# Contiguous stationary operands for the row maxima, and the row of maxima sent in four transfers

## The chip, the cores and the metric

The kernel runs on one core of a Trainium2 chip. The metric is the device time of one execution in microseconds (us). Before the change the median of three runs is 927.35 us (926.88 to 927.9).

## What is computed

An attention with queries pooled in pairs, followed by a two-layer block with a squared ReLU. Cut to what matters:

```
q, k, v: (4, 8, 1152, 64)
q_pool = q.reshape(B, H, S // 2, 2, D).mean(axis=3)
scores = scale * q_pool @ k^T
scores = scores - max(scores, axis=-1)
attn = exp(scores); attn = attn / (attn.sum(-1) + 1e-9)
x = (attn @ v), heads side by side: (2304, 512)
h = x @ w_in; r = maximum(h, 0); g = s * r * r + b
out = g @ w_out: (2304, 512)
```

There are 32 heads (4 batches of 8). The change touches only the maxima that are subtracted from the scores: one number for each of the 576 pooled queries of each head.

## The kernel before, in words

The work has two stages. The attention goes over 16 pairs of heads and takes somewhat more than the first half of the span; the two-layer block follows. The order of the work is written out by hand: a loop over 288 steps (32 heads of 9 blocks of 128 keys), in which strings of letters say in which order a step's score products, value products and maximum products are issued.

In a step, `score_step` (line 740) makes the scores of 128 keys against the 576 queries of a head: four matmuls on TensorE (PE), two for each half of the queries. In the first of the two the high parts are multiplied, and the second adds the low parts and, through one row of `qq` that meets a row of -1 in `kk`, subtracts the maxima. ScalarE (ACT) takes the exponentials (L749, L752), VectorE (DVE) or GpSimd (POOL) makes their low parts (L755), and `value_step` (L772 to L782) multiplies them with the values three steps later.

The maxima of a pair of heads are made while the pair before is worked on, by `max_unit`: 27 products for a pair, each of 128 queries against 384 keys, one PE matmul (L685) and one DVE reduction (L686). The stationary operand (the weights of the matmul) is a block of queries. In three of the 27 products it is `qm`, the last 64 queries of both heads; in the other 24 it is a quarter of `qz`, which holds the first 512 queries of one head with zeros beside them. For the first two pairs `qz` is written in an order in which a quarter is 128 neighbouring columns. From the third pair on a transfer copies `qh` into `qz` as it is (L591), and a quarter is read with a step of four columns of four bytes: quarter t holds the queries t, t + 4, t + 8 and so on. So the maxima of partition m lie beside one another in `pm` in the order of the queries.

When a head's maxima are complete, `shift` reduces them to `c` (L720 on DVE), and one tick later two transfers carry `c` into the row of `qq` that the second score matmul reads: the first 512 (L725, 128 partitions of four elements) and the last 64 (L726). Both are issued from the queue of SyncE (SP), which issues its transfers in the order of the program: a transfer that has to wait for its data holds up all that stand behind it. In the same queue stand the loads of raw keys and queries of the pair three further on (L546, L554), the copies of `kh`, `kT`, `qh` and `qT` into `kk` and `qq` (L609 to L630), the loads of the values (L559), the queries for the maxima (L591), the weights of the second stage (L202) and the results (L821). Twice in a pair the queue comes to a row of maxima.

Below, "the row" of a head is this row of maxima, and heads are counted from 0: head 4 is the first of the third pair.

Of the kernel before, what the change touches and what calls it, by code (L numbers as in the profile page):

```python
# [56 lines left out]
def f32(ap):  # L57
    return ap.bitcast(F32)
# [3 lines left out]
def attention_moe_kernel(ctx: ExitStack, tc: tile.TileContext, q, k, v, w_in, w_out, s_in, b_in, out):  # L62
    nc = tc.nc
    B, H, S, D = q.shape
# [4 lines left out]
    P = 128  # L69
# [3 lines left out]
    NT4 = SQ // P  # L73
# [228 lines left out]
    def later(k, fn):  # L302
        step[1] += 1
        queue.append((step[0] + k, step[1], fn))
# [215 lines left out]
    qzs = [ap.tile([P, 2, NT4 * P], F32R, name=f"qz{i}") for i in range(2)]  # L520
# [148 lines left out]
    def max_unit(u, pool, tag):  # L669

        p, w = divmod(u, NU)
        t, e = divmod(w, NE) if u >= (NT4 + 1) * NE else divmod(w, NT4 + 1)[::-1]
        if w == 0:
            pms[p] = ap.tile([P, NJ, NE], F32, tag="pm", bufs=2, name=f"pm{p}")
        h = 0 if t <= NT4 else 1
        ps = pool.tile([P, 512], F32, tag=tag, name=f"m{p}_{w}") if tag == "m" else pool.tile([P, 2, 512], F32, tag=tag, name=f"m{p}_{w}")[:, 0]
        if t == 0:
            assert holds["qm"] == p  # L680
            st, col = qm, NT4
        else:
            st = qzs[p % 2][:, h].rearrange(*(("p (m t) -> p t m",) if p > 1 else ("p (t m) -> p t m",)), t=NT4)[:, (t - 1) % NT4]
            col = (t - 1) % NT4 + h * (NT4 + 1)
        nc.tensor.matmul(ps[:, :KB], st, khs[p][:, e * KB:(e + 1) * KB], start=True, stop=True)  # L685
        nc.vector.tensor_reduce(out=pms[p][:, col, e:e + 1], in_=ps[:, :KB], axis=AX.X, op=ALU.max)  # L686
        if e == NE - 1 and t and t % NT4 == 0:
            pm = pms[p] if h == 0 else pms.pop(p)
            shift(2 * p + h, pm[:, h * NT4:(h + 1) * NT4 + 1], slice(0, NT4) if h == 0 else slice(1, NT4 + 1), NT4 if h == 0 else 0)
# [10 lines left out]
    def shift(hd, pm, full, rest):  # L700


        if hd == 0:
            turned = ap.tile([P, (NT4 + 1) * 32], F32, name="turned")
            nc.vector.tensor_reduce(out=first.rearrange("p (t i) -> p t i", i=32)[:, :, 0], in_=pm, axis=AX.X, op=ALU.max)
            nc.vector.transpose(out=turned, in_=first)
            flat = qqs[0].rearrange("p i a n -> p (i a n)")[D:D + 1, NT4 * P:].rearrange("p (t q i) -> p t q i", q=4, i=32)
            for g in range(4):
                at = flat[:, 0:NT4 + 1, g + 2] if g < 2 else flat[:, 1:NT4 + 1, g - 2]
                src = turned[32 * g:32 * g + 1].rearrange("p (t i) -> p t i", i=32)[:, :NT4 + 1 if g < 2 else NT4]  # L710
                if g % 2:
                    nc.scalar.activation(at, src, AF.Copy)
                else:
                    nc.vector.scalar_tensor_tensor(out=at, in0=src, scalar=1.0, in1=src, op0=ALU.mult, op1=ALU.max)
            holds["c", 0] = 0
            return
        c = ap.tile([P, 32], F32R, tag="c", bufs=2, name=f"c{hd}")[:, :NT4 + 1]
        row = qqs[hd % 3][:, 1].rearrange("p a n -> p (a n)")
        h = hd % 2
        nc.vector.tensor_reduce(out=c, in_=pm, axis=AX.X, op=ALU.max)  # L720

        eng = nc.sync

        def send():
            eng.dma_start(f32(row[D:D + 1, :NT4 * P]), f32(c[:, full]))  # L725
            eng.dma_start(f32(row[D:D + 1, NT4 * P:]), f32(c[h * D:(h + 1) * D, rest:rest + 1]))  # L726
            holds["c", hd % 3] = hd

        later(1, send)
# [136 lines left out]
    for n in range(AHEAD):  # L866
        for u in range(begun(n - AHEAD), begun(n - AHEAD + 1)):
            max_unit(u, *((ps_m, "m") if u % 2 == 0 else (ps_s, "s")))
            if u == 1:
                prep["qz1"]()  # L870
                load_q(1, (1,))
                load_k(1)
                load_q(1, (0,))
                prep["l1"]()
                zeros(1)
                constants(1)
                prep_v(0)
                ones(1)
                constants(2)
        tick()  # L880
        if n == 11:
            prep = prep_pair(1)
# [6 lines left out]
    for n in range(NS + LAG):  # L889
        hd, j = divmod(n, NJ)  # L890
# [4 lines left out]
        for part in ORDS.get(n % 18, ORD[at]) if at is not None else "sff":  # L895
            if part == "s" and n < NS:
                score_step(hd, j, KIND[n % 18])
            elif part == "f":
                for u in units:
                    max_unit(u, ps_m, "m")  # L900
                    break
            elif part == "v":
                if products is None:
                    products = value_step(*divmod(n - LAG, NJ))
                next(products)
# [3 lines left out]
        if n < NS:  # L909
            p, h = divmod(hd, 2)  # L910
# [150 lines left out]
```

## Time and profile before

| | |
|---|---|
| median of the runs | 927.35 us (926.88 to 927.9) |
| the profiled execution's own time | 927.01 us |
| its span, first to last instruction | 925.0 us |
| mean granted TensorE clock | 0.999 |
| PE matmul busy | 901.7 us (97%) |
| DVE, ACT, POOL busy | 692.1, 649.3, 631.0 us |
| matmuls of the maxima, L685 | 432 |
| transfers of rows of maxima, L725 and L726 | 31 and 31 |

Busy time of PE is modelled from the ends of its matmuls, which overlap, so 97% says that PE seldom stood without a matmul, not that it ran at its best. What one matmul costs is better read from the start of the one behind it. The weight loads are listed apart, as PEld; they lie beside the matmuls before them. "SPq" rows are transfers being issued: their length is the time in which SP was busy with the issue, and the landing comes later.

### The profile page before, as it was taken

The numbers are of one execution on the slowest core, as the hardware profiler recorded it, in microseconds if no ns is written. First come the engines' busy times: TensorE is split into PE (matmuls) and PEld (weight loads), VectorE is DVE, ScalarE is ACT, GpSimd is POOL, SyncE is SP. The second block draws the span as 40 slices with busy tenths as digits, with TensorE's granted clock in tenths as the row PEclk, the third lists the DMA queues.
The fourth block names the chain that finished last, engine by engine and source line by source line (L and its number), as shares of the span: only waits on it lengthen the run. The fifth ranks groups of instructions, "written<-read, shape, count | busy, mean of one in ns | idle before, by whom it ended". The sixth has DMA issues, their size and how long they took to land.

```text
span 925.0 us, 17875 instructions
## 1 busy us (share of the span) xinstructions
PE 901.7 (97%) x6164; PEld 864.3 (93%) x6164; DVE 692.1 (75%) x1272; ACT 649.3 (70%) x1209; POOL 631.0 (68%) x503
## 2 busy tenths in 40 slices
PE   5999999999999999999999999999999999999997
PEld 3898999999999999999998899989999999999997
DVE  6877878888888888888876587788884556666656
ACT  4878788888888888888888776756664444454443
POOL 7966866777777777777757566659997345555543
PEclk9999999999999999999999999999999999999999
DMA  9799887887788778777671367656653322222111
GB/s 162 152 183 194 181 185 147 174 182 175 152 176 181 172 149 186 174 172 150 140 177 50 124 186 227 216 158 219 205 167 109 114 69 69 69 70 69 47 47 46
DMA packets 257977, 134.65 MB, mean 146 GB/s; under 512 B 204192, under 2 KB 227872, under 8 KB 257888
## 3 DMA queue, kind: packets, MB, share of 16 engines
q1 hardware_dynamic: 250784, 132.63, 59.5%
q10 hardware_dynamic: 7104, 0.89, 0.6%
q8 instruction: 50, 0.82, 0.4%
q14 instruction: 39, 0.32, 0.1%
HBM read 68.68 MB, written 18.87 MB: 95 GB/s over the span
## 4 chain that ended last, share of the span: by engine, by line
PE 89%; POOL 3%; DMA 2%; DVE 2%; ACT 2%; issue 1%; SPq 0%; ACTq 0%; POOLq 0%; DVEq 0%
PE s L740 15%; PE h L412 11%; PE y L387 11%; PE h L360 10%; PE m L685 10%; PE seven L456 10%; PE o L778 7%; PE o L782 7%; PE o L780 6%; PE o L772 3%; POOL pl L755 1%; DMA kraw<-in_k_dram 1%; DMA kk<-kh 1%; ACT ph L749 0%; DMA qraw<-in_q_dram 0%
## 5 line engine op out<-in xcount | busy, mean ns | idle before, releaser
L686 DVE TENSOR_REDUCE pm<-m 128x1 f32<-128x384 f32 x432 | 230.8, 548 | 65.4 <-PE m L685 53.7
L755 POOL TENSOR_TENSOR pl<-pe,ph 128x576 fp32r<-128x576 f32 x128 | 182.0, 1432 | 103.2 <-ACT pe L752 77.1
L749 ACT ACTIVATE ph<-s 128x576 fp32r<-128x576 f32 x256 | 166.3, 650 | 73.3 <-PE s L740 67.7
L740 PE MATMUL s<-qq,kk 128*128 128x288 f32 x1152 | 202.4, 297 | 4.7 <-DVE pl L755 2.4
L740 PEld LDWEIGHTS s<-qq,kk 128*128 128x128 f32 x1152 | 174.4, 190 | 8.4 <-issue 1.9
L685 PE MATMUL m<-kh,qz 128*128 128x384 f32 x384 | 171.4, 454 | 0.3 <-DVE pm L686 0.3
L782 PE MATMUL o<-pl,vv 128*128 128x288 f32 x512 | 151.2, 295 | 1.2 <-POOL pl L755 1.2
L780 PE MATMUL o<-ph,vl 128*128 128x288 f32 (+1 forms) x512 | 150.9, 295 | 0.3 <-POOL vl L660 0.3
L778 PE MATMUL o<-ph,vv 128*128 128x288 f32 x512 | 150.8, 295 | 0.0
L685 PEld LDWEIGHTS m<-kh,qz 128*128 128x128 f32 x384 | 115.1, 300 | 5.4 <-DVE pm L686 2.3
L755 DVE TENSOR_TENSOR pl<-s,ph 128x576 fp32r<-128x576 f32 x128 | 96.4, 753 | 29.0 <-ACT s L752 22.1
L360 PE MATMUL h<-x,wih 128*128 128x256 f32 x576 | 106.8, 283 | 1.1 <-DVE gl L374 1.0
L412 PE MATMUL h<-x,wih 128*128 128x256 f32 x576 | 104.2, 281 | 0.0
L782 PEld LDWEIGHTS o<-pl,vv 128*128 128x128 f32 x512 | 96.7, 189 | 6.8 <-POOL pl L755 1.5
L360 PEld LDWEIGHTS h<-x,wih 128*128 128x128 f32 x576 | 93.7, 190 | 8.0 <-DVE gl L374 2.2
L778 PEld LDWEIGHTS o<-ph,vv 128*128 128x128 f32 x512 | 97.0, 190 | 0.0
L440 POOL TENSOR_TENSOR cl<-c,ch 128x640 fp32r<-128x640 f32 x35 | 55.0, 1571 | 56.3 <-ACT ch L436 56.3
L412 PEld LDWEIGHTS h<-x,wih 128*128 128x128 f32 x576 | 88.7, 188 | 0.2
L780 PEld LDWEIGHTS o<-ph,vl 128*128 128x128 f32 (+1 forms) x512 | 86.3, 169 | 0.6 <-POOL vl L660 0.6
L752 ACT ACTIVATE s<-s 128x576 f32<-128x576 f32 x128 | 83.1, 649 | 0.0
L752 ACT ACTIVATE pe<-s 128x576 f32<-128x576 f32 x128 | 82.9, 648 | 0.0
L360 PE MATMUL h<-x,wil 128*128 128x256 f32 x288 | 81.6, 283 | 0.0
(294 smaller groups left out, 2058.4 us busy)
## 6 DMA issues: line engine op xcount, KB each, us to landing
kk<-kh SPq DMA_DIRECT2D x31, 576.0 KB, 6.5
vf<-in_v_dram SPq DMA_DIRECT2D x32, 288.0 KB, 3.9
qq<-qh SPq DMA_DIRECT2D x64, 144.0 KB, 6.1
xr<-xd SPq DMA_DIRECT2D x18, 512.0 KB, 3.8
kk<-kT SPq DMA_DIRECT2D x31, 288.0 KB, 4.4
qraw<-in_q_dram SPq DMA_DIRECT2D x120, 72.0 KB, 2.5
kraw<-in_k_dram SPq DMA_DIRECT2D x60, 144.0 KB, 3.1
wsti<-in_moe_w_in_dram SPq DMA_DIRECT2D x13, 512.0 KB, 4.0
```

Of the source, the lines that this page charges most:

```text
L360: nc.tensor.matmul(h[:, :TB], st[:, c, :], mv[:, c, :], start=(n == 0), stop=(n == 3 * NC - 1))
L387: nc.tensor.matmul(y[:, :DM], st[:, ts_], mv, start=(first and n == 0), stop=(last and n == 2))
L412: nc.tensor.matmul(h[:, e * TB:(e + 1) * TB], st[:, c, :], mv[:, c, :], start=(k == 0), stop=(k == 3 * NC - 1))
L685: nc.tensor.matmul(ps[:, :KB], st, khs[p][:, e * KB:(e + 1) * KB], start=True, stop=True)
L686: nc.vector.tensor_reduce(out=pms[p][:, col, e:e + 1], in_=ps[:, :KB], axis=AX.X, op=ALU.max)
L740: nc.tensor.matmul(ps[:, a, :HALF], kk[:, i, j * P:(j + 1) * P], qq[:, i, a], start=(i == 0), stop=(i == 1))
L749: nc.scalar.activation(ph, ps[:, :, :HALF], AF.Exp, scale=SCALE)
L752: nc.scalar.activation(full, ps[:, :, :HALF], AF.Exp, scale=SCALE)
L755: fresh.append(lambda: eng.tensor_tensor(out=pl, in0=full, in1=f32(ph), op=ALU.subtract))
L778: nc.tensor.matmul(o[:, :HALF], vv[:, j], ph[:, a], start=first, stop=False)
L780: nc.tensor.matmul(o[0:vl.shape[2], :HALF], vl[:, j], ph[:, a], start=False, stop=False)
L782: nc.tensor.matmul(o[:, :HALF], vv[:, j], pl[:, a], start=False, stop=last)
```

## The change

The quarter of `qz` is now 128 neighbouring columns, so quarter t holds the queries 128 t to 128 t + 127. Nothing is changed in what fills `qz`: the first two pairs keep their reordered copy, the others get the queries in their natural order. In `c`, column t then holds the maxima of 128 neighbouring queries, one in each partition. From head 4 on the row is therefore sent in four transfers of 128 elements of four bytes, one for each column; the transfer of the last 64 stays as it was. Heads 1 to 3 keep their one transfer (head 0 has another way).

```diff
@@ max_unit
-            st = qzs[p % 2][:, h].rearrange(*(("p (m t) -> p t m",) if p > 1 else ("p (t m) -> p t m",)), t=NT4)[:, (t - 1) % NT4]
+            st = qzs[p % 2][:, h, (t - 1) % NT4 * P:((t - 1) % NT4 + 1) * P]
@@ shift, send
-            eng.dma_start(f32(row[D:D + 1, :NT4 * P]), f32(c[:, full]))
+            if hd < 4:
+                eng.dma_start(f32(row[D:D + 1, :NT4 * P]), f32(c[:, full]))
+            else:
+                for t in range(NT4):
+                    eng.dma_start(f32(row[D:D + 1, t * P:(t + 1) * P]), f32(c[:, full.start + t:full.start + t + 1]))
             eng.dma_start(f32(row[D:D + 1, NT4 * P:]), f32(c[h * D:(h + 1) * D, rest:rest + 1]))
```

On PE, DVE, ACT and POOL the instructions stand in the order in which they stood. The SP queue gets three more transfers for each of 28 heads, 84 in all. This is the queue at heads 4 and 5, where it changes first; `kraw` and `qraw` are raw keys and queries, `qz` the queries for the maxima (the numbers behind names are the program's own and shift by themselves):

```order
-L725 DMA qq_98<-c_1036 1x128x4
-L726 DMA qq_98<-c_1036 1x64x1
-L546 DMA kraw_1088<-in_k_dram 32x36x32 x4
-L554 DMA qraw_1093<-in_q_dram 32x18x32 x8
+L729 DMA qq_98<-c_1036 1x128x1 x4
+L730 DMA qq_98<-c_1036 1x64x1
+L546 DMA kraw_1091<-in_k_dram 32x36x32 x4
+L554 DMA qraw_1096<-in_q_dram 32x18x32 x8
 L591 DMA qz_102<-qh_961 64x512 x2
-L725 DMA qq_99<-c_1235 1x128x4
-L726 DMA qq_99<-c_1235 1x64x1
```

Everything behind a row, here the raw loads and `qz`, now stands behind three more transfers. The second place is one pair in the queue of the changed kernel, from the row of an even head (8) over the one of the odd head (9) to the load of values behind it (`wsti` is a weight of the second stage, `vf` the values):

```order
L729 DMA qq_99<-c_1934 1x128x1 x4
L730 DMA qq_99<-c_1934 1x64x1
L546 DMA kraw_1989<-in_k_dram 32x36x32 x4
L554 DMA qraw_1994<-in_q_dram 32x18x32 x8
L591 DMA qz_102<-qh_1859 64x512 x2
L202 DMA wsti0b<-in_moe_w_in_dram 128x2x256
L729 DMA qq_97<-c_2144 1x128x1 x4
L730 DMA qq_97<-c_2144 1x64x1
L559 DMA vf_104<-in_v_dram 128x9x64
```

The values of an odd head stand directly behind that head's row, and behind them (not shown) the copies into `kk` and `qq` for the next pair; these too are three transfers later.

## Rows read from the trace of the kernel before

**Rows 1.** Windows: length, busy PE, PEld, DVE, ACT, POOL, clock, DMA share, GB/s

```profile
50.76:85.05 34.29, 31.69 (x206) 30.32 (x205) 25.64 (x47) 25.37 (x47) 22.60 (x16) 1.00 0.93 193
...
333.75:364.83 31.08, 31.08 (x205) 30.46 (x204) 25.88 (x49) 26.32 (x50) 23.63 (x19) 1.00 0.81 169
```

**Rows 2.** Line 685, 62 to 494.5 us: count, duration min/median/max in ns

```profile
L685 PEld LDWEIGHTS m<-kh,qz x335: 308/309/314, 62.6 to 494.1; 128*128 128x128 f32 x168
...
L685 PEld LDWEIGHTS m<-kh,qm x39: 187/188/188, 91.0 to 466.0; 128*128 128x128 f32 x39
```

**Rows 3.** Timeline of PE (start, length in us): second pair's quarter, then a later one

```profile
43.26 0.33 PE L685 MATMUL m<-kh,qz 128*128 128x384 f32 x1
43.43 0.29 PE L778 MATMUL o<-ph,vv 128*128 128x288 f32 x1
...
253.09 0.43 PE L685 MATMUL m<-kh,qz 128*128 128x384 f32 x1
253.36 0.30 PE L782 MATMUL o<-pl,vv 128*128 128x288 f32 x1
```

**Rows 4.** Timeline of PE: the same behind an L772 matmul, second pair, then a later one

```profile
44.28 0.55 PE L685 MATMUL m<-kh,qz 128*128 128x384 f32 x1
44.67 0.69 PE L740 MATMUL s<-qq,kk 128*128 128x288 f32 x4
...
358.18 0.55 PE L685 MATMUL m<-kh,qz 128*128 128x384 f32 x1
358.57 0.69 PE L740 MATMUL s<-qq,kk 128*128 128x288 f32 x4
```

**Rows 5.** Timeline of the SP queue: start, length of the issue

```profile
336.74 0.54 SPq L202 DMA_DIRECT2D wsto1b<-in_moe_w_out_dram  x1
340.10 0.51 SPq L725 DMA_DIRECT2D qq<-c  x1
340.65 0.59 SPq L726 DMA_DIRECT2D qq<-c  x1
341.34 0.54 SPq L559 DMA_DIRECT2D vf<-in_v_dram  x1
...
357.03 0.51 SPq L725 DMA_DIRECT2D qq<-c  x1
```

**Rows 6.** Waits of the SP queue, 81 to 450.3 us: total, times, longest

```profile
SPq L725 <- DVE c L720: 44.8, 24, 3.5
SPq L612 <- PE m L685: 5.6, 15, 0.8
```

**Rows 7.** Lines 725 and 726, whole span: issue in ns min/median/max; landing of L726

```profile
L725 SPq DMA_DIRECT2D qq<-c x31: 482/510/1344, 29.6 to 495.5; - x31
...
L726 SPq DMA_DIRECT2D qq<-c x31: 588/594/1397, 30.2 to 496.1; - x31
...
DMA to landing us min/median/max: 1.8/1.8/3.1
```

**Rows 8.** Timeline of PE: the first score matmuls of heads 4 and 22

```profile
85.05 0.69 PE L740 MATMUL s<-qq,kk 128*128 128x288 f32 x4
...
364.83 0.69 PE L740 MATMUL s<-qq,kk 128*128 128x288 f32 x4
```

**Rows 9.** Waits of PE, 50.76 to 92 us

```profile
PE s L740 <- DMA qq<-c: 0.7, 1, 0.7
```

**Rows 10.** Timeline of SP: the last transfer of the row of head 4

```profile
81.79 0.59 SPq L726 DMA_DIRECT2D qq<-c  x1
```

**Rows 11.** Timeline of ACT: values of heads 3 and 21 rounded, idle time before in brackets

```profile
70.45 0.69 ACT L293 ACTIVATE vv<-vf 128x576 fp32r<-128x576 f32 x1 [3.24 <-DMA vf<-in_v_dram]
...
349.32 0.69 ACT L293 ACTIVATE vv<-vf 128x576 fp32r<-128x576 f32 x1
```

**Rows 12.** DMA issues of the page: size, median us to landing

```profile
vf<-in_v_dram SPq DMA_DIRECT2D x32, 288.0 KB, 3.9
```

**Rows 13.** DMA queue of the page: packets, MB, share of 16 engines' span

```profile
q1 hardware_dynamic: 250784, 132.63, 59.5%
```

## The prediction, made before the changed kernel was run

> **What bounds the kernel now.** I read the windows first, because shares of the whole span mix two stages and the change lies in the attention alone. In a pair from the middle, PE is busy for all of 31.08 us [rows 1]; ACT has 26.32, DVE 25.88, POOL 23.63, and the transfers take 0.81 of the 16 DMA engines. So PE sets the pace of a pair, with some 5 us to spare on the others. In the second pair PE stands idle for 2.6 of 34.29 us, 0.7 of it for a row of maxima [rows 1, 9].
>
> Then I looked at line 685 by stationary operand. A load of `qm`, which is contiguous, takes 188 ns; one of a strided quarter of `qz` takes 309 [rows 2]. Loads lie beside matmuls, so their length alone says little. The timeline gives the price: from a strided product to the next matmul PE takes 0.27 us; from the same product in the second pair, where the quarter is contiguous, 0.17 [rows 3].
>
> Last I read the SP queue, the only one that the change lengthens. It is nearly as full as PE. From one row to the next, 340.10 to 357.03, it issues without a long pause; ahead of the row at 340.10 it stands from 337.28 on, for its data [rows 5]. From head 4 to head 28 it waits 44.8 us in 24 waits for `c` [rows 6], 1.9 us for a head, and this is nearly all the room that it has.
>
> **What the change takes away.** 14 pairs have 24 strided products each, 336. Not all of them gain. Three in a pair stand between an L772 matmul and a score matmul, and there the step is 0.39 us with the contiguous quarter too (44.28 to 44.67) as with the strided one (358.18 to 358.57) [rows 4]: the load is not what is waited for. I cost these 42 at nothing. The other 21 in a pair gain 0.27 - 0.17 = 0.10 us: 2.1 us for a pair, which would then take 29.0. ACT would be busy for 26.3 of these, DVE for 25.9: tight, but not the bound. If only PE mattered, the pairs behind head 4 would give 13 x 2.1 = 27 us.
>
> The row shows the strided load 121 ns dearer than the contiguous one. The Trainium skill, page "SBUF — State Buffer", section "Door 1: The DMA port swizzle", gives 4 fp32 as the step that is still free, which is this step; by that sentence the change would take nothing away. The trace does not agree: 309 against 188 ns.
>
> **What it adds.** Three transfers for each of 28 heads, all on SP. The trace of before has none of 128 elements of four bytes. Its neighbours are L725 (128 partitions, 0.51 us to issue) and L726 (four-byte elements, 0.59 us) [rows 7]; from one start to the next it is 0.55 and, by the two transfers behind 340.65, at most 0.69 [rows 5]. I take 0.60, the new one being like the one in its partitions and like the other in its elements: a = 1.8 us for a head, 3.6 for a pair. The ends are 0.55 (a = 1.65) and 0.69 (a = 2.07). Nothing covers this but the waits of SP itself.
>
> On the DMA engines a row becomes 512 packets instead of 128: 768 more in a pair. At the mean of the queue, 0.595 x 925 x 16 / 250784 = 35 ns a packet [rows 13], these are 1.7 us of the 16 engines in a pair, an upper bound since the mean holds packets of kilobytes. With 0.81 x 31.08 = 25.2 us that makes 26.9 of 29.0. I cost it at nothing; PE and SP cover it.
>
> **The sum.** In a pair SP had 3.7 us of waits for `c` and gets 3.6 us of issues, while PE wants to be 2.1 us faster. Both can't be had: SP becomes the bound, and the rows arrive late, where now they arrive early. Head 22 shows how early: its last transfer leaves at 357.59 (0.56 behind L725), lands 1.8 us later at 359.4, and the head begins at 364.83 [rows 5, 7, 8]: 5.4 us of slack. Once this is used up, PE waits at the even heads until the row has landed.
>
> So I follow SP. Up to the row of head 4 I take it as full, since PE was short of a row there already [rows 9], and nothing moves. From there to head 28 it loses its waits and gains the issues: 44.8 + 2 - 24 x 1.8 = 3.6 us earlier. The 2 are my estimate for the waits on buffers that PE frees, of which L612 alone has 5.6 [rows 6]; an SP that is late meets fewer of them. The row of head 28 lands 3.6 - 1.8 earlier, and PE, with no slack left, starts the head 5.4 + 1.8 = 7.2 us earlier than now. Behind that SP has no raw loads any more, and PE gains the 2.1 us of the last pair's products. Together 9.3 us; the second stage just starts so much sooner. At head 4 itself PE loses: the last transfer left at 81.79 [rows 10], leaves 1.8 us later and lands at 85.4 to 86.7 by the ends of its landing time [rows 7], where the head began at 85.05 [rows 8]. That loss is inside the count, since SP is what is followed.
>
> Against the profiled execution, 927.0 us, this gives 917.7; I say **918**. The median of the runs is 0.3 above that execution, well inside the range. In short the gain is 54.3 - 25 a: 13 us at a = 1.65, 2.5 at 2.07, and 2 less where the other waits do not shrink. The forecast's own range is 908 to 926.
>
> What is late next: the values of an odd head stand behind its row. At head 21 they leave at 341.34, land 3.9 us later at 345.2 and are rounded by ACT at 349.32 [rows 5, 11, 12]: 4.1 us of slack, which loses 1.8 and then what SP is late. How it looks when it is gone stands at 70.45, where ACT idles 3.24 us for it [rows 11]. I expect a microsecond there at odd heads, paid out of the wait that PE would have at the next even head.
>
> **The rivals.**
> *PE stays the bound.* If SP's smaller waits, on buffers that PE frees, vanish as well, or the added issues come at the cheap end, SP keeps up. For it: L612 is only one of several lines that wait so. Against it: by the formula a would have to be 1.1, or 0.37 a transfer, unless some 18 us of such waits go. Then the full 27 us come, less 1 at head 4: about 901.
>
> *The added issues cost more than the two neighbours.* It turns at 54.3 = 25 a, that is a = 2.17, 0.72 us for an added transfer. For it: both lines have issues of 1.3 and 1.4 us [rows 7], when the queue ahead of them is full, and an SP that never pauses will find it full more often; in the second pair, with a DMA share of 0.93, PE was already short of a row [rows 1, 9]. Against it: the medians lie close to the minima. With 0.9 us a transfer, between 0.6 and 1.2, a is 2.7 and the kernel is 13 us slower, 940.
>
> *The loads don't get faster*, because the step is not what makes them slow. For it: the strided loads also follow transfers into `qz`, those of the first two pairs do not. Against it: the same line, shape and engine, with 188 ns in the second pair's step of 0.17. Then PE keeps 31.08 a pair, SP fits under it with 3.6 for 3.7 us, and the wait at head 4 remains: 928. The sentence on the step in the Trainium skill, page "SBUF — State Buffer", cited above, would give this outcome.
>
> **How the numbers follow.** Forecast 53 in 100, PE as the bound 25, dearer issues 16, unchanged loads 6. A measurement of this kernel can tell 0.2%, 1.9 us, from no change. Faster by more than that are nearly all of the forecast's cases and all of the first rival's, less a few at the forecast's upper end: 0.73. Within it: the unchanged loads and those few, 0.11. Slower: 0.16. The range runs from 899, to take in most of the first rival, up to 927, the upper end of the forecast and a little of the third; the dearer issues are left out, with bits of the others, 2 in 10.
>
> **What would show it.** In the changed profile: loads of line 685 near 188 ns for all quarters, and 0.17 us to the next matmul (if not, the third rival). Issues of the added transfers at 0.51 to 0.65 us. Waits of SP for `c` nearly gone from 100 to 430 us, and in their place waits of PE for the transfer of a row at even heads, about 1 us each; a pair of some 30.5 us there (31.08 less 7.2 / 12) and of 29.0 near the end. If PE still never waits and a pair takes 29.0, the first rival holds. If a pair takes over 31.1, with issues of 0.7 us and more, the second does. The forecast is wrong as a whole if PE waits for something else: for DVE or ACT at the faster pace, for instance.

## The result, and the profile after

The changed kernel takes 931.95 us (median of 6 runs, 930.85 to 934.82), the kernel before 926.64 in the same session (6 runs, 925.96 to 927.9). The ratio is 1.0058, with a 95% interval of 1.0042 to 1.0073: slower by 0.6%, where 918 was forecast and 927 was the end of the range. The profiled execution took 932.1 us with a span of 930.3; that of before took 927.0 with a span of 925.0. One of the four executions of the run with the four transfers alone, below, took 1070.55 us at a mean granted clock of 0.757 and is left out there.

**PE is no longer busy through a pair.** The windows of the changed kernel, with the columns of [rows 1]: the pair behind head 4, a pair from the middle, and the one behind head 28, the first in which SP has no raw loads to issue.

```profile
84.32:115.60 31.28, 29.89 (x207) 28.53 (x205) 25.35 (x46) 26.41 (x48) 21.71 (x16) 1.00 0.80 161
304.97:336.44 31.47, 30.03 (x206) 28.45 (x204) 25.48 (x49) 26.17 (x50) 23.71 (x19) 1.00 0.82 168
464.26:493.43 29.17, 29.17 (x205) 28.28 (x204) 23.89 (x46) 24.80 (x46) 18.38 (x16) 1.00 0.70 156
```

Before, a middle pair was 31.08 us long and PE busy for all of it [rows 1]. Now PE works 1 us less and stands still for 1.4; the pair is longer. From the start of head 4 at 84.32 to that of head 28 at 464.26 the 12 pairs take 31.66 us on average. Where SP is relieved, the pair falls to 29.17, the 29.0 of the forecast.

**The loads did what was forecast.** Line 685 by form in the changed kernel, 62 to 494.5 us, answering to [rows 2]:

```profile
L685 PEld LDWEIGHTS m<-kh,qz x330: 186/188/330, 62.5 to 492.3; 128*128 128x128 f32 x165
...
L685 PEld LDWEIGHTS m<-kh,qm x39: 187/188/188, 90.7 to 471.9; 128*128 128x128 f32 x39
```

PE's timeline, answering to [rows 3, 4]: start, length.

```profile
252.84 0.55 PE L685 MATMUL m<-kh,qz 128*128 128x384 f32 x1
253.23 0.69 PE L744 MATMUL s<-qq,kk 128*128 128x288 f32 x4
...
254.29 0.34 PE L685 MATMUL m<-kh,qz 128*128 128x384 f32 x1
254.46 0.30 PE L784 MATMUL o<-ph,vl 128*64 128x288 f32 x1
```

The load is 188 ns instead of 309, the step to the next matmul 0.17 us instead of 0.27, and behind an L776 matmul (L772 before) still 0.39.

**The issues are not what was forecast.** The row of maxima on the SP queue, with the columns of [rows 7]:

```profile
L729 SPq DMA_DIRECT2D qq<-c x112: 472/593/1537, 80.3 to 502.8; - x112
...
DMA to landing us min/median/max: 1.9/2.9/5.7
...
L730 SPq DMA_DIRECT2D qq<-c x31: 592/600/1866, 30.4 to 503.5; - x31
...
DMA to landing us min/median/max: 1.8/2.2/3.4
```

The median is the 0.60 that I took, but I took it for a whole step from one start to the next, and between two issues lie another 0.046 us: 0.64. What SP pays is the sum. My sum over the issue records from the row of head 4 to that of head 28 gives 48 row transfers with 28.51 us before and 120 with 78.14 now, 49.6 more. The 72 added ones, the second to the fourth of each row, have 43.9 of that, 0.61 each. The other 5.8 lie in the two transfers of a row that stood there before: over all heads the first takes 3.4 us more than L725 did, the one of the last 64 queries 2.3 more than L726. With the gaps between issues, 3.3 us more in all, the 24 heads pay 53.0 us, so **a is 2.21 us** a head, where 1.8 was taken and 2.07 was the upper end: 1.97 for the added transfers with their gaps, 0.24 for the two beside them. The SP timeline shows a row at the odd head 21, then one at the even head 22:

```profile
346.37 0.53 SPq L202 DMA_DIRECT2D wsto1b<-in_moe_w_out_dram  x1
347.00 2.44 SPq L729 DMA_DIRECT2D qq<-c  x4
349.48 0.60 SPq L730 DMA_DIRECT2D qq<-c  x1
...
363.68 0.62 SPq L559 DMA_DIRECT2D vf<-in_v_dram  x1
364.40 2.88 SPq L729 DMA_DIRECT2D qq<-c  x4
367.33 0.60 SPq L730 DMA_DIRECT2D qq<-c  x1
...
364.40 0.95 SPq L729 DMA_DIRECT2D qq<-c  x1
```

At head 21 the four go out in 2.44 us, as the medians would have it. At head 22 they take 2.88, because the first alone takes 0.95 (the last line, from a narrower stretch). At both heads the row follows the load before it within 0.1 us, where SP stood still from 337.28 to 340.10 before [rows 5]. The first transfer is dearer at the even heads alone, where it stands behind the load of values (L559): 0.81 us in the mean of 12 heads, against 0.53 before, and 0.51 at the odd heads in both kernels. In the kernel before, it took 0.51 or 0.52 at the 11 even heads where SP had stood still for more than a quarter of a microsecond ahead of it, and 0.69 at head 4, the one without a pause. So the missing pause and the longer issue go together there; what in the queue makes the issue longer no run isolates.

**SP has nothing left to give.** Its waits, 80 to 458.7 us, with the columns of [rows 6]:

```profile
SPq L729 <- DVE pm L686: 8.0, 17, 0.9
...
SPq L612 <- PE m L685: 4.4, 6, 1.6
```

The 44.8 us for `c` [rows 6] are gone. The 8.0 us now put down to line 686 are no wait for maxima: at head 22 DVE had written `c` by 361.03 (360.86 and 0.17 for it), more than 3 us before the row left. By the starts and ends of the issue records SP stands idle ahead of the rows for 2.4 us in all, 0.1 a row, where it was 46.8. Followed as in the forecast, from the row of head 4 to that of head 28, SP takes 378.30 us where it took 369.25: 53.0 added by the rows, 44.4 of waits removed, and all its other lines together the same to about half a microsecond.

**So the rows arrive late**, and PE waits at the even heads, as the forecast said it would. PE's waits from 85 to 500 us, and its timeline at head 22:

```profile
PE s L744 <- DMA qq<-c: 13.8, 13, 2.0
PE m L685 <- DVE pm L686: 2.0, 8, 0.3
```

```profile
368.44 0.29 PE L744 MATMUL s<-qq,kk 128*128 128x288 f32 x1
369.75 0.70 PE L744 MATMUL s<-qq,kk 128*128 128x288 f32 x3 [1.02 <-DMA qq<-c]
```

These are 13 waits of about a microsecond, at the even heads from 4 to 26 and at head 30. By head 22 the lateness has added up: the head begins at 368.44, not at 364.83 [rows 8], and then waits another 1.02 us for its row. ACT's waits from 85 to 460 us show the second thing that was to come late, the values behind the rows:

```profile
ACT vv L293 <- DMA vf<-in_v_dram: 13.3, 16, 1.8
```

Ten of these 16 waits, 10.6 us of the 13.3, lie at odd heads.

### The profile page after: what moved, and what is told of

It reads as the page before. It is cut to its first block, busy times and chain, and to the rows that moved or that the text cites. A ratio compares the mean times of both kernels' runs of the same rounds, so it can differ in the third digit from the quotient of the medians.

```text
span 930.3 us, 18028 instructions
## 1 busy us (share of the span) xinstructions
PE 889.5 (96%) x6164; PEld 838.0 (90%) x6164; DVE 686.9 (74%) x1272; ACT 647.6 (70%) x1209; POOL 631.2 (68%) x503
## 3 DMA queue, kind: packets, MB, share of 16 engines
q1 hardware_dynamic: 262880, 132.63, 60.2%
## 5 line engine op out<-in xcount | busy, mean ns | idle before, releaser
L686 DVE TENSOR_REDUCE pm<-m 128x1 f32<-128x384 f32 x432 | 227.6, 546 | 59.8 <-PE m L685 54.8
L744 PE MATMUL s<-qq,kk 128*128 128x288 f32 x1152 | 211.3, 303 | 20.5 <-DMA qq<-c 14.0
L685 PE MATMUL m<-kh,qz 128*128 128x384 f32 x384 | 144.8, 384 | 2.7 <-DVE pm L686 2.3
L685 PEld LDWEIGHTS m<-kh,qz 128*128 128x128 f32 x384 | 74.4, 194 | 12.4 <-DVE pm L686 6.7
L784 PEld LDWEIGHTS o<-ph,vl 128*128 128x128 f32 (+1 forms) x512 | 82.9, 162 | 0.0
```

Of the source, the lines that this page charges most:

```text
L744: nc.tensor.matmul(ps[:, a, :HALF], kk[:, i, j * P:(j + 1) * P], qq[:, i, a], start=(i == 0), stop=(i == 1))
L784: nc.tensor.matmul(o[0:vl.shape[2], :HALF], vl[:, j], ph[:, a], start=False, stop=False)
```

## The experiments

Four theories were to be told apart. **A**: the added issues fill the SP queue, the rows leave late. **B**: PE would be fast enough, but DVE or ACT can't follow a pair of 29 us. **C**: the row is late because its smaller transfers take longer to land. **D**: the number of packets slows the other transfers. Each run was timed beside the kernel before on the same chip (926.49 us in the first four, 926.02 in the others). The ratios are those on record and can differ from the quotient of the medians by a tenth of a per cent.

**The faster loads alone.** The four transfers are taken back; the quarters stay contiguous.

```diff
-            if hd < 4:
-                eng.dma_start(f32(row[D:D + 1, :NT4 * P]), f32(c[:, full]))
-            else:
-                for t in range(NT4):
-                    eng.dma_start(...)
+            eng.dma_start(f32(row[D:D + 1, :NT4 * P]), f32(c[:, full]))
```

> The contiguous quarters of the change, with the one transfer of before for every row; the row so holds the maxima of its queries in another order (that part of the computation is changed). Theory A (the added issues on SP take back what the loads give): SP has 26.6 us of work in a pair, PE needs 29.0, so PE sets the pace and the 13 pairs behind head 4 gain about 27 us: 897 to 904 us, a pair of 29.0 us, and PE does not wait for rows. Rival B (the faster loads can't be used, because DVE and ACT don't follow at 29.0 us a pair): 915 to 927 us, with waits of PE for DVE in place of those for rows.

Measured: 901.35 us, ratio 0.9729 (0.9715 to 0.9744). A window of one pair, and SP's wait for `c` from 81 to 450 us:

```profile
288.79:317.95 29.16, 29.16 (x205) 28.27 (x204) 25.68 (x49) 25.90 (x50) 23.68 (x20) 1.00 0.91 188
```

```profile
SPq L725 <- DVE c L720: 19.7, 13, 5.5
```

PE is busy for every one of the 29.16 us and waits for nothing from 85 to 470 us. DVE with 25.68 and ACT with 25.90 follow it: B falls. The gain of 25 us is the 27 of the forecast's first rival less two. SP, asked to do the same work in 29.16 us a pair, pays for it out of its waits. The row of head 28 leaves at 427.6 here; up to there SP keeps 14.2 us of its 44.8 us of waits for `c`, and one wait of 5.5 us lies behind. From the row of head 4 to that of head 28 it takes 346.6 us instead of 369.25. Its idle time ahead of the rows falls by 30.4 us: 22.6 went into the shorter pairs, 7.8 into issues that took longer. One of these is the row's own transfer, which is the same as before the change:

```profile
L725 SPq DMA_DIRECT2D qq<-c x31: 482/603/1219, 29.9 to 469.8; - x31
```

Its median is 0.603 us where it was 0.510 [rows 7]; at the even heads its mean is 0.71 where it was 0.53. So an issue gets longer in a queue with fewer pauses, without any added transfer.

**The four transfers alone.** The stride of four comes back; the row goes out in four transfers, each now holding every fourth query.

```diff
-            st = qzs[p % 2][:, h, (t - 1) % NT4 * P:((t - 1) % NT4 + 1) * P]
+            st = qzs[p % 2][:, h].rearrange(*(("p (m t) -> p t m",) if p > 1 else ("p (t m) -> p t m",)), t=NT4)[:, (t - 1) % NT4]
```

> The four transfers alone: the quarters keep their step of four columns (the row is then laid in another order than its queries; that part of the computation is changed). Theory A: PE wants 31.1 us a pair and SP needs about 31.7, so SP still sets the pace: 929 to 935 us, about as the change itself, with row waits of PE at even heads. Rival B (the transfers fit under PE; what is lost in the change is lost by the contiguous loads): 926 to 928 us, no waits for rows.

Measured: 933.42 us (median of three, 933.3 to 935.09), ratio 1.0084 (1.0064 to 1.0104). PE's waits from 85 to 500 us:

```profile
PE s L744 <- DMA qq<-c: 3.5, 4, 1.4
```

Up to head 12 a pair still takes 31.09 us, the added issues paid out of SP's waits and the rows' slack; behind it 31.1 to 32.8. So the four transfers cost 7 us beside slow loads and 31 beside fast ones (931.95 against 901.35). Read the other way, the loads are worth 25 us with one transfer and some 2 with four, which the two intervals don't tell from nothing. The two halves of the change draw on the same room, SP's waits; that is A.

**Seven transfers.** Three of the four are sent a second time, so that only the number of issues changes.

```diff
-                for t in range(NT4):
+                for t in (*range(NT4), *range(NT4 - 1)):
```

> The change with three more transfers of a row, sending its first three quarters twice. Theory A: 84 more issues of 0.59 us and gaps of 0.05 us on the queue that sets the pace, about 1.9 us a head: 54 us on top of 932, so 975 to 995 us. Rival C (what holds PE is the time in which a row lands, not the queue): a later landing by 1.9 us at each even head only, 932 to 960 us.

Measured: 1005.15 us (two runs), ratio 1.085 (1.0828 to 1.0872): some 20 us beyond the expectation's middle and 10 beyond its end. First SP's waits from 85 to 530 us, then PE's from 85 to 560:

```profile
SPq L729 <- DMA qq<-c: 19.9, 21, 2.3
```

```profile
PE s L744 <- DMA qq<-c: 47.7, 13, 4.2
PE s L744 <- DVE pl L759: 8.1, 8, 1.5
```

The second copy of a quarter writes where the first one writes and waits until it has landed: 19.9 us that I had not counted, besides 72 issues. PE waits for rows 47.7 us instead of 13.8, and the granted clock from 85 to 560 us is 0.93 in the mean, with stretches at 0.5, the level of 1.2 GHz; in the windows shown here it is 1.00. From the row of head 4 to that of head 28 SP takes 440.1 us, 61.8 more than in the change, 37.4 of it in the issues of the rows and 27.6 between them. The direction is A's, but what of the time is the waits' and what the clock's is not separated, so the size is no clean measure of an issue.

**Half the stride, half the transfers.** A quarter is read with a step of two, and the row goes out in two transfers of 256 elements.

```diff
-            st = qzs[p % 2][:, h, (t - 1) % NT4 * P:((t - 1) % NT4 + 1) * P]
+            g = (t - 1) % NT4
+            st = qzs[p % 2][:, h, g * P:(g + 1) * P] if p < 2 else qzs[p % 2][:, h, g // 2 * 2 * P:(g // 2 + 1) * 2 * P].rearrange("p (m s) -> p s m", s=2)[:, g % 2]
...
-                for t in range(NT4):
-                    eng.dma_start(f32(row[D:D + 1, t * P:(t + 1) * P]), f32(c[:, full.start + t:full.start + t + 1]))
+                for t in range(0, NT4, 2):
+                    eng.dma_start(f32(row[D:D + 1, t * P:(t + 2) * P]), f32(c[:, full.start + t:full.start + t + 2]))
```

> Quarters with a step of two columns from the third pair on, so that two neighbouring maxima stay together and a row goes out in two transfers of 128 x 2 elements. If a step of two loads like a contiguous one (188 ns): SP has one added issue a head, 28.0 us a pair, below the 29.0 of PE, and by theory A nearly all of the gain comes: 898 to 908 us. If it loads like the step of four (309 ns): PE keeps 31.1 us a pair, SP stays below it, 926 to 929 us. Rival B (DVE and ACT don't follow): 915 to 927 us with loads of 188 ns.

Measured: 902.07 us, ratio 0.9735 (0.972 to 0.9749). Its loads (line 686 here), a window of one pair, and the issues of the row:

```profile
L686 PEld LDWEIGHTS m<-kh,qz x335: 193/195/199, 62.7 to 469.8; 128*128 128x128 f32 x168
```

```profile
319.42:348.59 29.17, 29.17 (x206) 28.31 (x204) 25.65 (x49) 25.91 (x50) 23.87 (x20) 1.00 0.88 183
```

```profile
L730 SPq DMA_DIRECT2D qq<-c x56: 472/592/1605, 81.3 to 471.6; - x56
```

A step of two costs a load 7 ns, a step of four 121. One added transfer a head still fits under a pair of 29.17 us; three don't. This kernel computes all of the reference and **beats both**: 24 us faster than before, 30 faster than the change.

**One transfer of 512 elements.** The maxima are kept two columns apart, so that no two elements of a packet lie together and one transfer carries as many elements as the four of the change.

```diff
-        c = ap.tile([P, 32], F32R, tag="c", bufs=2, name=f"c{hd}")[:, :NT4 + 1]
+        c = ap.tile([P, 32], F32R, tag="c", bufs=2, name=f"c{hd}")
+        c = c[:, :2 * (NT4 + 1):2] if hd >= 4 else c[:, :NT4 + 1]
...
-            if hd < 4:
-                eng.dma_start(f32(row[D:D + 1, :NT4 * P]), f32(c[:, full]))
-            else:
-                for t in range(NT4):
-                    eng.dma_start(...)
+            eng.dma_start(f32(row[D:D + 1, :NT4 * P]), f32(c[:, full]))
```

> Contiguous quarters, and one transfer of 512 elements of four bytes for a row: c is written with a step of two, so that its four maxima are four elements (the row holds the maxima of its queries in another order; that part of the computation is changed). As many small packets as in the change, but one issue. Theory A (issues on the SP queue): about as with one transfer of 128 x 4, 899 to 905 us, with an issue near 0.5 to 0.65 us. Rival D (it is the number of elements or packets that costs): an issue of 2 us and more, or 925 to 935 us.

Measured: 903.63 us, ratio 0.9761 (0.9746 to 0.9775). The issues, and how long they took to land:

```profile
L726 SPq DMA_DIRECT2D qq<-c x31: 523/682/1756, 29.3 to 471.3; - x31
...
DMA to landing us min/median/max: 1.9/4.8/6.7
```

The row lands in 4.8 us, longer than the 2.9 of a quarter in the change, and the pair takes 29.16 us all the same, with 0.7 us of waits of PE for a row from 85 to 470 us. So a later landing costs no time here, and C falls; D falls as what made the change slow, but the elements are not free. The issue itself is 0.68 us, 0.08 more than in the run with one transfer of 128 x 4. SP pays again behind the row, at the even heads, where the raw keys follow. Their issues from 81 to 430 us:

```profile
L546 SPq DMA_DIRECT2D kraw<-in_k_dram x48: 560/754/3108, 81.2 to 405.1; - x48
```

The second load behind the row takes 1.7 us in the mean instead of 0.6, and all 48 together 53.9 where they take 33.5 in the run with one transfer of 128 x 4 (median 0.607): 1.7 us a pair. Together with the row's own issue that leaves SP no wait ahead of a row beyond 0.1 us, and the pair of 29.16 just fits. In the change the same loads took 32.8; there this price was not paid.

**Other issues moved off SP.** The change, with the two loads of `qz` in a pair issued by GpSimd.

```diff
             if p > 1:
-                nc.sync.dma_start(f32(to), of)
+                nc.gpsimd.dma_start(f32(to), of)
```

> The change, with the two transfers of queries for the maxima (qz) issued from GpSimd instead of SP; the rows are as in the change. Theory A: SP loses two issues of 0.66 us a pair, the pair goes from about 31.7 to 30.4 us, 12 such pairs make 15 us: 912 to 922 us, and the waits of PE for rows shrink. Rival C (the landing of four small transfers is what holds PE): 929 to 933 us, since the rows are untouched.

Measured: 918.71 us, ratio 0.9935 (0.9913 to 0.9957), inside the expectation. A window of one pair, and PE's waits from 85 to 470 us:

```profile
297.44:328.11 30.67, 29.64 (x206) 28.33 (x204) 25.55 (x49) 26.10 (x50) 24.70 (x21) 1.00 0.86 172
```

```profile
PE s L744 <- DMA qq<-c: 10.2, 14, 1.5
```

The row's own transfers are as in the change. Two issues fewer on SP, for other data, take 13 us off. From head 4 (82.59) to head 28 (448.48) a pair takes 30.49 us on average instead of 31.66, so one issue in a pair is worth 0.59 us to that pair. Of all runs this one says most directly that it is the fullness of the queue, not the row's transfers as such.

**The three added transfers on ACT.**

```diff
-                    eng.dma_start(...)
+                    (eng if t == 0 else nc.scalar).dma_start(...)
```

> The change, with three of the four transfers of a row issued from ScalarE. Theory A: SP is back at 26.6 us a pair plus small change; ACT has 26.3 us a pair and gets six issues of about 0.6 us, 29.9, and so becomes the bound by a little: 903 to 916 us. Rival C (landing): 929 to 933 us.

Measured: 988.87 us, ratio 1.0685 (1.0665 to 1.0705), a plain miss: the fast end of A had said 903. SP's waits from 85 to 470 us, then PE's:

```profile
SPq L554 <- DMA qq<-c: 90.6, 14, 10.4
SPq L546 <- DMA qq<-c: 9.5, 18, 1.8
```

```profile
PE m L685 <- DMA qz<-qh: 22.5, 11, 2.6
PE s L744 <- DVE pl L759: 20.5, 10, 2.8
```

SP, relieved of the issues, waits 90.6 us at L554, the raw loads of the queries, until a row transfer has landed; it has nothing to do with these loads' data. In this run's trace the transfers of SP and of ACT count on the same eight completion semaphores, those of GpSimd, in other runs, on eight of their own. At each of the 14 waits the load waits on the very semaphore that it is to count on itself, and what ends the wait is the landing of a transfer that ACT had issued on it. ACT, with work of its own, issues its transfers late, and SP inherits the delay. No run with other semaphores was tried. The granted clock was 0.97 in the mean from 85 to 560 us, and what that adds is not separated. The run says nothing against A and nothing for it.

**The three added transfers on GpSimd.** The same edit, with `nc.gpsimd` for `nc.scalar`.

> The change, with three of the four transfers of a row issued from GpSimd, which has 23.6 us a pair; what an issue costs there no trace has shown. Theory A: SP is relieved as before; if an issue takes GpSimd under 0.9 us, PE sets the pace: 900 to 906 us; if it takes more, 906 to 920. Rival C (landing): 929 to 933 us.

Measured: 908.43 us, ratio 0.981 (0.9795 to 0.9825), 2 us beyond the expectation for a cheap issue. The issues, and how long all four took to land:

```profile
L729 POOL DMA_DIRECT2D qq<-c x84: 537/539/717, 77.4 to 473.4; - x84
...
L729 SPq DMA_DIRECT2D qq<-c x28: 483/510/1492, 80.8 to 472.0; - x28
...
DMA to landing us min/median/max: 1.9/4.2/6.0
```

A pair takes 29.33 us and PE waits for nothing from 85 to 470 us. The same four transfers, landing in the same place and later than in the change (4.2 us in the median instead of 2.9), cost 7 us more than one transfer instead of 31; and most of those 7 are not even in the pairs. Its last score matmul ends at 494.3 us, within 1 us of the kernel with two transfers (493.4), whose span is 5.7 us shorter (900.8 against 906.5). The last output transfers are issued 0.9 us apart in the two (898.07 and 897.14), so about 5 us lie behind the last work. The trace shows what they are, a DRAIN of GpSimd at the end of the program:

```profile
L1061 POOLq DRAIN  x3: 40/98/8310, 897.4 to 906.2; - x3
```

The longest of these three takes 8.31 us, with 84 transfers issued by GpSimd; with the 28 of the run above, where `qz` was moved, it is 3.73, and in the kernel with two transfers, with none, 1.43. Here SP is through at 901.1, and the DRAIN runs to 905.7; with 28 transfers it ends about when SP does. Why it grows with the transfers is not shown.

## Why the prediction was wrong, point by point

- *What bounds the kernel* was right: PE before, with SP nearly as full behind it. That the sum has to follow SP was right too. Without that I should have said 901, and the change would have looked like a failure of the loads.
- *What the change takes away* was right: 188 ns, 0.17 us, 0.39 where the load is hidden, 29.17 us for a pair where PE is free to run, 25 us in the run with the loads alone. The Trainium skill, page "SBUF — State Buffer", section "Door 1: The DMA port swizzle", gives 4 fp32 as how far one can stride for free, and a step of four is not free here: the runs show 188, 195 and 309 ns at steps of one, two and four, and the last is what the 25 us come from. The same note of the Trainium skill also asks for at least two accesses to each 16-byte line, which a step of two fp32 makes and a step of four does not; with that the three numbers agree.
- *What it adds* is **the step that failed: "I take 0.60 ... a = 1.8 us for a head".** It measured 2.21, outside both ends. The added transfers themselves stayed inside them: 0.61 us and the gap of 0.046, 0.66 a step, so 1.97 a head where I had 1.8. What the term left at nothing, without a reason, is that the two transfers that stood in a row already would take longer: 0.24 a head. At 1.97 the forecast's formula still gives a kernel that is 5 us faster; at 2.21 it gives one that is 1 us slower. I had taken medians from a queue with 45 us of pauses in it, for a queue that would have none. The run with one transfer shows an unchanged transfer at 0.603 instead of 0.510 us where two thirds of the pauses are gone; by what mechanism was not tried. The row that warned of it stood there (issues of 1.3 and 1.4 us, [rows 7]), and I used it for a rival only. That term alone makes 24 x 0.41 = 9.8 us, and the 25th row 0.4. The packets that I cost at nothing were 864 more in a pair, not 768 (262880 on the page in place of 250784); the run with 512 elements in one transfer has 768 more (261536) and takes 903.63 us, so they are not what cost the change its time.
- *What SP gets back* was too large by 2.4: 44.4 where I wrote 44.8 + 2. The other waits did not shrink; by line some grew and some shrank, and the sum stayed to about half a microsecond.
- *The end of the chain*: the forecast's own steps with these two terms give +3.3 us instead of -9.3. The measured step between the two profiled executions is +5.1. The rest is small. The row of head 4, which I held fixed, left 0.8 us earlier (80.28 for 81.04), and SP's other lines took 0.5 more. At head 22 PE has its row 5.35 us after the first of its transfers leaves (364.40 to 369.75), before 2.37 (357.03 to 359.4), which is 0.8 beyond a, the last pieces landing in 2.2 us and more instead of 1.8. The 1.3 us that are left were not followed; in this execution the granted clock stood at 0.50 from 434.7 to 438.1, just behind PE's longest wait for a row (1.98 us, up to 433.54).
- *The rivals.* What came is the second, "the added issues cost more than the two neighbours". It was to turn at 0.72 us for an added transfer, and it measured 0.74 with the whole of a put on the three. The rival's reason, a queue without pauses, has the rows above on its side; that the queue was full no row shows. I had given it 16 in 100, and priced it at 0.9 us and 940; between its turning point and that price lies the result. The case was nearer than its chance said: the forecast's own upper end, 0.69, was 0.03 from the point at which the sign changes.
- *What would show it.* Waits for `c` gone, waits of PE for rows at even heads of about 1 us, waits of ACT for values at odd heads of about 1 us (10.6 us in ten): all came. The pair of 30.5 us did not; it was 31.66, and the forecast's text names "over 31.1" as the sign of the second rival.

## What to carry to other kernels

A queue that issues transfers is an engine with a length per stage: add up its issues, compare with the stage, and treat its waits as the budget of every edit that adds a transfer or shortens the stage, since both draw on it. Price an issue by its mean with the gap behind it, and not by a median, and expect the issues beside it to get longer when the queue loses its pauses; when the break-even lies close to an end of the price, say so in the chances. An edit that pays in issues may be had for fewer: here a step of two instead of one kept nearly all of the gain for a third of the added transfers.

## What the runs showed that I had not expected

- The cost of a strided stationary operand is not even in the step: 188 ns contiguous, 195 at a step of two, 309 at a step of four (128x128, four-byte elements).
- The time to issue hardly depends on the elements in a transfer itself, the landing does: 512 separate elements in one transfer issue in 0.68 us and land in 4.8; a quarter of them issues in 0.59 and lands in 2.9. The queue paid for the 512 later, in the second load behind them, with 1.7 us instead of 0.6.
- GpSimd issued its transfers in 0.54 us with a largest value of 0.72, steadier than SP's 0.59 with 1.54, and paid at the end of the program, with a DRAIN of 8.31 us behind 84 transfers. Moving an issue to ACT instead held up SP for 90.6 us, by waits on transfers that its loads had no use for.
- Sending a piece of a row twice made the second transfer wait for the first to land, 19.9 us in all.
